# Products that nobody reads, issued in TensorE's planned pauses

## The chip, the cores and the metric

The kernel runs on one core of a Trainium2 chip. The metric is the device time of one launch in microseconds (us); the reference point is the median of three runs. A core has five engines that run side by side, each taking its own instructions in order: TensorE (PE; its weight loads are the row PEld), VectorE (DVE), ScalarE (ACT), GpSimd (POOL) and SyncE (SP), which issues the DMAs. TensorE's clock is granted by a throttle: the profile gives it as a share of full speed.

## What is computed

A gated complex linear attention, followed by a two-layer network with a Gelu. The inputs are f32, but for `w_in` and `w_out`, which arrive as 64-bit floats; the result is f32:

```python
q, k, v, a_re, a_im: (4, 8, 768, 48)          # batch, heads, time, head_dim
mag = sqrt(a_re**2 + a_im**2); scale = minimum(mag, 0.999) / (mag + 1e-6)
for t in range(768):                          # S: (4, 8, 48, 48), complex
    S = (a_re + 1j * a_im)[t] * scale[t] * S  # row by row
    S.real += k[t] outer v[t]
    y[t] = q[t] @ S.real
x = y as (3072, 384)
out = gelu(x @ w_in) @ w_out                  # (384, 2048), (2048, 384)
```

## The kernel before

**The work has four kinds of parts**, all written as steps into one plan.

- *Lanes.* The decays are normalised and multiplied up along time, in 24 slices over four groups of time steps. This is mostly VectorE's and ScalarE's, with the tiles `a`, `tab`, `bt`, `tt` and `xt`. The scaled keys and queries go through DRAM (`kq`). In the first slices TensorE adds up the squares (`sum_of`: `att<-tab` and `att<-a`).
- *Weights.* 32 pieces of 384 columns. The inputs are 64-bit floats, and each piece is split into a high part (`wi_hi`, `wo_hi`) and a low part (`wi_lo`, `wo_lo`). TensorE forms the low part in PSUM, as `ident * wh - hi - lo`: three products, the first in f32, in the profile `po<-wh,ident_r`, `po<-wi_hi,minus` and `po<-wi_lo,minus` (or the same with `wo`). ScalarE or VectorE copies the sum out (`wi_lo<-po`). The PSUM tile is always the same one, columns 0 to 383 of `pos[2]`. The next piece's first product can start when the copy is over. The buffers `wh` are two.
- *Units.* 24 of them, each 128 time steps of one batch: keys and queries are turned by TensorE (`att<-ident_r,kqn`), copied out (`kp`, `qT`), multiplied to scores (`att<-qT,kp`), masked by VectorE (`kp<-att,causal`) and multiplied with `vn`; the state is brought forward with products of 64 by 64 (`ph<-vn,kqn`). At its end ScalarE (`xT`, `x`) and VectorE split the unit's output into high and low parts. Ahead of unit 0, and as steps of unit 0, TensorE turns the ends of the first lane group (`gains`: `att<-ident_r,vw`).
- *Blocks.* Nine blocks j0 to j8 of two or three units (256 or 384 columns): the two layers, each as three products of high and low parts (`ph<-xT,wi_hi`, `po<-wo_hi,gh` and so on), with two Gelus per tile on ScalarE (`gh`, `gf`) and their difference on VectorE (`gl`).

**PSUM** has eight banks, all taken: three `att`, two `ph`, three `po` (`pos`). Block j0 has two units and uses `pos[0]` and `pos[1]`; block j1 has three and uses `pos[2]` too. A weight piece and a block's sum take 384 of a bank's 512 columns.

**The order.** Nothing of the order is written by hand. `Plan.add` records each step with its cost on its engine, and with the steps that it must follow. `Plan.order` runs through the steps forward and backward with these costs, keeps the best order, and leaves in each step its engine, the start that the plan gives it (`s.start`, us) and its cost (`s.cost`). `Plan.issue` then emits the instructions of all engines in that order. In the plan TensorE's cost doubles for 4 us (`WARM`) behind a pause of over 3 us (`COLD`). The waits between engines are put in when the program is built, from which instruction reads or writes what, in program order.

The plan's times are estimates; on the chip each engine runs its instructions as soon as what they wait for is there. A pause in the plan is the difference between one TensorE step's `s.start` and the end of the step before it on TensorE.

## Time and profile before

| | |
|---|---|
| median of 3 runs | 697.37 us (697.04 to 699.15) |
| the profiled execution | 697.16 us, of which the span of its instructions 695.1 us |
| mean granted TensorE clock | 0.957 |
| busy over the span | TensorE 92%, weight loads 85%, VectorE 67%, ScalarE 66%, GpSimd 5% |
| chain that ended last | TensorE 75%, ScalarE 11%, VectorE 10% |

How to read it: every helper's instruction carries the line of `Plan.issue` (L399), so groups are told apart by their tiles, `out<-in`. `x2` counts instructions; an f32 product is two of them, a product of the rounded kind (fp32r) one. In a time-line each row has the start, the busy time, the engine, the operation with its tiles and sizes, and in brackets the idle time ahead of it and what ended it. In a table of windows each row has the stretch, its length, then for TensorE, weight loads, VectorE, ScalarE and GpSimd the busy us and the number of instructions, then the granted clock, the DMA share and GB/s. A matmul's end is modelled, so consecutive rows of TensorE can overlap; the spacing of their starts is the better measure.

### The profile page before, as it was taken

To read this page: it belongs to the slowest core of one execution; us is meant where nothing else is said; L and a number is where in the kernel's file an instruction comes from. 1 tells how busy PE (TensorE), PEld (TensorE's weight loads), DVE (VectorE), ACT (ScalarE), POOL (GpSimd) and SP (SyncE) were. 2 spreads that over 40 slices of the span, in tenths; PEclk is the share of its full clock that TensorE was granted. 3 is DMA by queue.
4 is the path that set the end of the run, shared out by engine and by line. 5 is a ranking of instruction groups with operands and counts; after the bars stand their busy time and mean duration, and the time that the engine had idled before them with its cause. 6 is when DMAs were issued, how large, how long until landed. Compare 5 with 4: busy or idle time off the path is not lost.

```text
span 695.1 us, 13858 instructions
## 1 busy us (share of the span) xinstructions
PE 638.8 (92%) x5138; PEld 588.3 (85%) x5138; DVE 465.7 (67%) x1154; ACT 459.3 (66%) x1118; POOL 31.9 (5%) x73
## 2 busy tenths in 40 slices
PE   3464799998999999999999999999999999999995
PEld 1232477996889999999889999999999999999995
DVE  5999988999999999999999973442332222131111
ACT  7777867999988788889899864454344333343332
POOL 1002110020000000300000000100000000000000
PEclk9865589999999999999999999999999999999998
DMA  8446936677455546637767555202322030010000
GB/s 303 138 136 176 301 110 165 203 199 234 134 150 148 148 119 183 180 95 217 206 198 212 118 133 149 83 20 72 113 76 61 5 103 1 1 44 4 24 1 26
DMA packets 112713, 86.68 MB, mean 125 GB/s; under 512 B 55680, under 2 KB 104960, under 8 KB 112640
## 3 DMA queue, kind: packets, MB, share of 16 engines
q1 hardware_dynamic: 112640, 85.75, 43.3%
q8 instruction: 41, 0.67, 0.4%
q14 instruction: 32, 0.26, 0.1%
HBM read 56.82 MB, written 23.59 MB: 116 GB/s over the span
## 4 chain that ended last, share of the span: by engine, by line
PE 75%; ACT 11%; DVE 10%; issue 2%; DMA 1%; SPq 0%; ACTq 0%; DVEq 0%
PE po L399 28%; PE ph L399 26%; PE att L399 20%; DVE a L399 2%; ACT tab L399 2%; DVE tt L399 1%; ACT wh L399 1%; ACT a L399 1%; DVE wh L399 1%; DVE xt L399 1%; ACT L399 1%; ACT L397 1%; DVE bt L399 1%; DVE tab L399 1%; ACT gh L399 1%
## 5 line engine op out<-in xcount | busy, mean ns | idle before, releaser
L399 PE MATMUL ph<-xT,wi_hi 128*128 128x384 f32 (+1 forms) x864 | 210.9, 326 | 0.3 <-ACT gf L399 0.3
L399 DVE TENSOR_TENSOR gl<-gf,gh 128x384 fp32r<-128x384 f32 (+1 forms) x143 | 72.9, 510 | 137.4 <-ACT gf L399 134.7
L399 PEld LDWEIGHTS ph<-xT,wi_hi 128*128 128x128 f32 x864 | 153.0, 188 | 3.1 <-ACT gf L399 0.6
L399 ACT ACTIVATE gh<-ph 128x384 fp32r<-128x384 f32 (+1 forms) x144 | 65.5, 455 | 134.3 <-PE ph L399 133.3
L399 PE MATMUL ph<-xT,wi_lo 128*128 128x384 f32 (+1 forms) x432 | 137.2, 318 | 1.8 <-ACT wi_lo L399 1.8
L399 PE MATMUL po<-wo_hi,gh 128*128 128x384 f32 x384 | 133.0, 346 | 1.1 <-ACT gh L399 0.9
L399 PE MATMUL po<-wo_lo,gh 128*128 128x384 f32 x384 | 129.6, 338 | 0.0
L399 PE MATMUL po<-wo_hi,gl 128*128 128x384 f32 x384 | 92.1, 341 | 0.3 <-DVE gl L399 0.3
L399 PEld LDWEIGHTS ph<-xT,wi_lo 128*128 128x128 f32 x432 | 81.2, 188 | 2.0 <-ACT wi_lo L399 2.0
L399 PEld LDWEIGHTS po<-wo_hi,gh 128*128 128x128 f32 x384 | 72.1, 188 | 3.4 <-ACT gh L399 2.5
L399 PEld LDWEIGHTS po<-wo_lo,gh 128*128 128x128 f32 x384 | 72.3, 188 | 0.1
L399 DVE TENSOR_TENSOR tt<-bt,a 128x192 f32<-128x192 f32 x192 | 69.0, 360 | 0.8
L399 PEld LDWEIGHTS po<-wo_hi,gl 128*128 128x128 f32 x384 | 65.9, 188 | 1.3 <-DVE gl L399 0.9
L399 ACT ACTIVATE gf<-ph 128x384 f32<-128x384 f32 (+1 forms) x144 | 65.0, 452 | 2.1 <-DVE gl L399 1.8
L399 PE MATMUL po<-wh,ident_r 128*128 128x384 f32 x64 | 35.4, 642 | 24.7 <-ACT wh L399 8.8
L399 PE MATMUL att<-qT,kp 96*128 96x128 f32 x384 | 53.4, 283 | 2.9 <-ACT kp L399 1.0
L399 DVE TENSOR_TENSOR kp<-att,causal 128x512 f32<-128x512 f32 x48 | 33.0, 687 | 30.8 <-PE att L399 30.0
L399 PEld LDWEIGHTS att<-qT,kp 96*128 96x128 f32 x384 | 48.8, 194 | 5.1 <-ACT qT L399 1.7
L399 DVE TENSOR_TENSOR bt<-tt 128x96 f32<-128x96 f32 x192 | 48.3, 251 | 0.9
L399 PEld LDWEIGHTS po<-wh,ident_r 128*128 128x128 f32 x64 | 12.6, 233 | 30.5 <-ACT wh L399 8.7
L399 PE MATMUL att<-ident_r,kqn 128*96 128x128 f32 x384 | 35.6, 237 | 0.3 <-DVE kp L399 0.2
L399 PEld LDWEIGHTS att<-ident_r,kqn 128*96 128x96 f32 x384 | 32.6, 127 | 3.1 <-DVE kp L399 0.5
(161 smaller groups left out, 1001.3 us busy)
## 6 DMA issues: line engine op xcount, KB each, us to landing
kqn<-kq SPq DMA_DIRECT2D x24, 768.0 KB, 5.1
xt<-in_x_lanes_dram SPq DMA_DIRECT2D x24, 384.0 KB, 3.7
kq<-xt SPq DMA_DIRECT2D x48, 192.0 KB, 3.8
kq<-xt SPq DMA_DIRECT2D x24, 384.0 KB, 4.1
a<-in_a_lanes_dram SPq DMA_DIRECT2D x20, 384.0 KB, 3.7
raw<-in_w_pieces_dram SPq DMA_DIRECT2D x16, 384.0 KB, 4.0
raw<-in_moe_w_out_dram SPq DMA_DIRECT2D x16, 384.0 KB, 3.9
vn<-in_v_units_dram SPq DMA_DIRECT2D x24, 256.0 KB, 5.4
```

What stands on the lines that cost most here:

```text
L397: self.nc.scalar.preload_act_table_set(table)
L399: getattr(getattr(self.nc, engine), name)(*args, **kw)
```

## The change

Three constants are new, and `issue` takes a function `unread`. As it walks through the order, it looks at each TensorE step whose planned start is later than `first`, until the first step of block j1. `first` is the planned start of the first TensorE step of the kind "units", less 14 us. Ahead of such a step it issues as many unread products as go into the planned pause, less 0.1 us, at 0.23 us each. A product is the f32 identity times itself, 128 by 128, added to columns 384 to 511 of `pos[2]`. These are set to zero once by VectorE, ahead of everything that the plan issues, and nothing reads them. The order of the other instructions on each engine stays as it was.

```diff
+SPARE, UNREAD, LEAD = 0.1, 0.23, 14.0
...
-    def issue(self):
+    def issue(self, unread):
+
+        free, early = 0.0, True
+        order = self.order()
+        first = min(s.start for s in order if s.engine == "tensor" and s.kind == "units") - LEAD
         table = FIRST_TABLE
         self.nc.scalar.preload_act_table_set(table)
-        for s in self.order():
+        for s in order:
             if s.table and s.table != table:
                 table = s.table
                 if table != "gelu":
                     self.nc.scalar.preload_act_table_set(table)
+            if s.engine == "tensor":
+                early = early and s.part != "j1"
+                for _ in range(int((s.start - free - SPARE) / UNREAD) if early and s.start > first else 0):
+                    unread()
+                free = s.start + s.cost
             for engine, name, args, kw in s.calls:
                 getattr(getattr(self.nc, engine), name)(*args, **kw)
...
-    P.issue()
+
+    unread = pos[BLK - 1][:, DM:512]
+    nc.vector.memset(unread, 0.0)
+    P.issue(lambda: nc.tensor.matmul(out=unread, lhsT=ident[:], rhs=ident[:], start=False, stop=False, skip_group_check=True))
```

## The prediction

> **What bounds the kernel now.** I read the cores first, then the windows of 10 us (for each engine the busy microseconds, then the granted TensorE clock, the DMA share, GB/s), then the time-lines of TensorE, ScalarE and VectorE around the first unit.

> ```profile
> core 0: 695.1 us, clock 0.957
> 0.00:10.00 10.00, 1.23 (x3) 0.84 (x3) 2.85 (x7) 8.83 (x21) 2.15 (x18) 1.00 0.78 265
> 60.00:70.00 10.00, 5.03 (x12) 2.55 (x10) 9.96 (x26) 7.77 (x19) 3.44 (x3) 0.50 0.73 202
> 70.00:80.00 10.00, 5.83 (x11) 2.67 (x10) 9.66 (x31) 7.48 (x21) 2.50 (x5) 0.50 1.01 291
> 80.00:90.00 10.00, 9.07 (x86) 7.69 (x87) 8.92 (x23) 8.73 (x21) 0.00 (x0) 0.50 0.75 237
> 90.00:100.00 10.00, 10.00 (x100) 7.37 (x99) 8.83 (x16) 5.88 (x16) 2.23 (x1) 0.88 0.24 73
> 130.00:140.00 10.00, 10.00 (x97) 8.59 (x96) 9.93 (x27) 9.84 (x23) 0.47 (x2) 1.00 0.43 120
> 200.00:250.00 50.00, 49.45 (x482) 46.92 (x482) 49.52 (x127) 43.42 (x98) 0.00 (x0) 1.00 0.58 152
> ```

> The reader is to see three stages. To about 88 us VectorE has no time free (9.96 and 9.66 of 10) and TensorE half of its time. From 80 to 100 TensorE is full, at half clock for most of it. From 130 TensorE and VectorE are both full, so a shift of both at 120 us should reach the end nearly whole, and a shift of one alone should not.

> Why the clock is low: TensorE works on weight pieces (one f32 product of 384 columns and two corrections each) with pauses between them.

> ```profile
> 49.86 2.93 PE L399 MATMUL att<-a,ident_r 128*128 128x384 f32 x4 [5.12 <-ACT a L399]
> ...
> 58.71 1.65 PE L399 MATMUL po<-wh,ident_r 128*128 128x384 f32 x2 [3.22 <-ACT wo_lo L399]
> 64.11 1.65 PE L399 MATMUL po<-wh,ident_r 128*128 128x384 f32 x2 [2.88 <-ACT wi_lo L399]
> 66.20 0.63 PE L399 MATMUL att<-ident_r,vw 128*96 128x128 f32 x2
> 68.92 1.62 PE L399 MATMUL po<-wh,ident_r 128*128 128x384 f32 x2 [2.10 <-DVE wh L399]
> 70.66 0.59 PE L399 MATMUL po<-wi_lo,minus 128*128 128x384 f32 x1
> 74.26 1.65 PE L399 MATMUL po<-wh,ident_r 128*128 128x384 f32 x2 [3.00 <-ACT wi_lo L399]
> 76.02 0.52 PE L399 MATMUL po<-wo_lo,minus 128*128 128x384 f32 x1
> 77.11 1.65 PE L399 MATMUL po<-wh,ident_r 128*128 128x384 f32 x2 [0.57 <-ACT wo_lo L399]
> 80.93 1.65 PE L399 MATMUL po<-wh,ident_r 128*128 128x384 f32 x2 [1.53 <-ACT wi_lo L399]
> 83.15 1.95 PE L399 MATMUL ph<-vn,kqn 64*64 64x48 f32 x32
> 87.92 2.07 PE L399 MATMUL att<-qT,kp 96*128 96x128 f32 x8
> 89.65 1.20 PE L399 MATMUL att<-ident_r,kqn 128*96 128x128 f32 x8
> ```

> I call the six pieces P1 (58.71), P2, P3, A (74.26), B and C. Five of the six pauses end with ScalarE's copy of the piece before out of its PSUM bank. VectorE pays for the low clock in these waits:

> ```profile
> 78.11 0.36 DVE L399 TENSOR_SCALAR wh<-raw 128x384 uint32<-128x384 uint32 x1 [0.34 <-ACT wh L399]
> 90.10 0.69 DVE L399 TENSOR_TENSOR kp<-att,causal 128x512 f32<-128x512 f32 x1 [1.12 <-PE att L399]
> 94.54 0.69 DVE L399 TENSOR_TENSOR kp<-att,causal 128x512 f32<-128x512 f32 x1 [0.80 <-PE att L399]
> 95.76 0.95 DVE L399 TENSOR_TENSOR m<-st,gg 96x768 f32<-96x768 f32 x1 [0.27 <-PE ph L399]
> 117.69 0.55 DVE L399 COPY st<-att 96x384 f32<-96x384 f32 x1 [1.69 <-PE att L399]
> ```

> All five are 4.2 us, and the four behind unit 0's start 3.9. Faster TensorE work cannot give more than this before 120 us: VectorE has nothing else to save.

> **The change part by part.** The memset of 128 columns is one VectorE instruction ahead of the lanes; VectorE works 2.85 of its first 10 us, so nothing. No DMA is added, nothing is moved, and nothing is queued on SP or POOL.

> Price of one product (f32, 128 by 128, two instructions as all f32 products here): the nearest rows are the scores, four products in eight instructions. At half clock the next work starts 1.73 us behind (87.92 to 89.65), 0.43 each; at full clock:

> ```profile
> 106.51 0.91 PE L399 MATMUL po<-wh,ident_r 128*128 128x384 f32 x2
> 107.71 0.43 PE L399 MATMUL ph<-qT,st 96*48 96x64 f32 x8
> 108.66 1.12 PE L399 MATMUL att<-qT,kp 96*128 96x128 f32 x8
> 109.72 1.13 PE L399 MATMUL ph<-vn,kqn 64*64 64x48 f32 x32
> ```

> 1.06 us, 0.265 each. The change counts 0.23, so a filled pause runs over by a seventh, and at half clock by nearly its own length. The first two rows give a piece at full clock, 1.20 us (106.51 to 107.71); at half clock it is 2.28 (74.26 to 76.54).

> How many: the pauses come from the plan, which the trace shows only through its outcome. "First unit" in the code is the first TensorE step of kind units; that is the transposes of the ends at 66.20, not the products at 83.15. 14 us before it is 52.2, so all six pauses are filled. With the measured pauses (pause less 0.1, by 0.23) they get 13, 12, 8, 12, 2 and 6, together 53. The upper end: a plan that counts pieces near 1.20 us has five pauses longer by some 1.1, 4 to 5 products each, some 76.

> Where they run: the products write columns 384 to 511 of the bank whose columns 0 to 383 hold the weight pieces. What two engines do in other columns of one bank is ordered here, as a unit's split shows: VectorE's xT reads columns 0 to 383 and needs only ScalarE's xT, yet it starts when ScalarE's read of columns 384 to 511 (x) is over:

> ```profile
> 562.84 0.49 ACT L399 ACTIVATE xT<-att 128x384 fp32r<-128x384 f32 x1 [1.74 <-PE att L399]
> 563.32 0.27 ACT L399 ACTIVATE x<-att 128x128 fp32r<-128x128 f32 x1
> 563.48 0.20 ACT L399 ACTIVATION_READ_ACCUMULATOR x<-att 128x1 f32 x1
> 563.71 0.56 DVE L399 TENSOR_TENSOR xT<-att,xT 128x384 fp32r<-128x384 f32 x1 [2.02 <-ACT x L399]
> ```

> So I take it that products issued ahead of a piece wait for ScalarE's copy of the piece before, the very event that ends the pause in five of six. They run behind the pause, and the piece is queued behind them. [...]

> What waits for the pieces is ScalarE, which takes its instructions in order:

> ```profile
> 63.60 0.46 ACT L399 CAST wi_lo<-po 128x384 fp32r<-128x384 f32 x1
> 66.89 0.46 ACT L399 CAST wo_lo<-po 128x384 fp32r<-128x384 f32 x1
> 73.75 0.45 ACT L399 CAST wi_lo<-po 128x384 fp32r<-128x384 f32 x1
> 75.94 0.58 ACT L399 ACTIVATE wh<-raw 128x384 f32<-128x384 f32 x1 [0.23 <-PE po L399]
> 78.85 0.56 ACT L399 ACTIVATE wh<-raw 128x384 f32<-128x384 f32 x1 [0.77 <-ACT wh L399]
> 80.41 0.46 ACT L399 CAST wi_lo<-po 128x384 fp32r<-128x384 f32 x1
> ```

> P1: the clock stands at 0.50 there, and the share of 0.88 from 90 to 100 puts its return at 92.4, 4.5 us behind the first full work of unit 0 (the scores at 87.92). So 10 products at 0.43 and 3 at 0.265 are 5.1 us, then 1.20: it ends at 65.0, and its copy stood at 63.60; ScalarE is 1.4 late. P2: 12 products are 3.2, the piece is 1.1 shorter, its copy at 66.89 has 0.5 of slack behind its end near 66.4 (the transposes behind it start at 66.20): 1.6 more, 3.0. P3: 8 are 2.1, and from its end at 71.25 to its copy at 73.75 there are 2.5: nothing. A: 12 are 3.2; the activation at 75.94 had waited for A's first product, 0.75 shorter at full clock: 2.4 more, 5.4. B: 2 are 0.5, against the same 0.75 at 78.85: 0.2 back, 5.2. C: 6 are 1.6, less 1.1: unit 0 starts 5.7 late, near 88.9. VectorE waits for ScalarE's wh at 78.11 already, so it is late with it: 5.2 less that 0.34, about 4.9. (Were VectorE's buffers to hide it all, this term would be zero; with the clock at half throughout, 53 products at 0.43 less those slacks would make it about 15.)

> What comes back is unit 0 at full clock: its 6.85 us from 83.15 to about 90.0 become 4.1 to 4.6 (the ratio of 1.73 to 1.06, and a little for ScalarE's copies between), so the scores are there at about 93.5, and VectorE, late itself, arrives at 93.9 (its wait began at 88.98, 90.10 less 1.12). The waits of 1.12, 0.80, 0.27 and, if the clock holds until then, 1.69 go: 3.9. What is late next is VectorE's own queue.

> From unit 0 to the second block more planned pauses are filled. The lower end is nothing, where a pause is real; the upper is 0.265 for each product where TensorE has no pause, as from 130 to 140. The pause left out of account by 0.1 and the seventh of overrun make a few tenths for each; I take five products, 1.3.

> Sum: 4.9 - 3.9 + 1.3 = 2.3 us on the profiled execution's 697.16, 699.4. That execution stands 0.2 under the median of the three runs, 697.37.

> **The rivals.** First, other side: the products do not wait for the copy and run inside the pauses. Then the 4.9 is gone and all 4.2 are gained, less overruns, of which I keep 1.2: 694.2. For it speaks that every pause is there in the trace and VectorE is full; against it the rows at 563. It decides if fewer than about half of the products before C stand behind the copies, since 3.9 then outweighs 2.5 and 1.3.

> Second: the plan's pauses are the long ones. 23 products more, 6.1 us, of which the slack of P3 and B's and C's waits take about 2: 703.5. The same comes out if 14 us before the transposes reaches the step at 49.86 too.

> Third: the products do run, but the clock does not hold through unit 0. TensorE was 9.07 of 10 us busy from 80 to 90 and stayed at 0.50, on transposes and 64 by 64 products. Without the 3.9 the time is 697.16 + 4.9 + 1.3 = 703.4. [...]

> Fourth: the filled pauses change nothing, TensorE being off the path until 74 us: delay and gain cancel, 697.2.

> **How the numbers follow.** A measurement of this kernel tells about 0.3% (2.1 us) from no change. The main case has 0.50; its own range is 697.3 to 701.5, half of it above 699.5: 0.25 slower, 0.25 within. The first rival has 0.27, all faster, 692.5 to 695.2. The second and third have 0.09 and 0.08, slower. The fourth has 0.06, within. So 0.27 faster, 0.31 same, 0.42 slower. The range reaches from inside the first rival to the second: 693.3 to 703.5.

> **What would show it.** Right: clock 1.00 from about 63 to past 120; products starting behind wi_lo and wo_lo, and the next piece right behind them; P1's copy near 65.0, A's activation near 81, unit 0's first product near 88.9; VectorE's waits near 90 to 97 and at 117 gone. Wrong: products that start at the end of the piece before; unit 0 at 83 or earlier; a clock of 0.50 anywhere from 65 to 120; TensorE late at the second block by more than VectorE.

## The result, and the profile after

The changed kernel takes 705.9 us (median of 4 runs, 704.79 to 708.95) against 697.67 (4 runs) for the kernel before: a ratio of 1.0122, with a 95% interval of 1.0085 to 1.0159, 8.2 us more. The forecast was 699.4.

The profiled execution, of 708.95 us, is the longest of the four, so shifts read from it are some 3 us larger than the median's. Its lines have the number L409 where the kernel before has L399, and the added products are L1026. Its cores view and some of its windows:

```profile
core 0: 706.8 us, clock 0.967
60.00:70.00 10.00, 9.43 (x60) 8.39 (x58) 7.67 (x20) 4.61 (x11) 3.38 (x2) 0.84 0.60 167
70.00:80.00 10.00, 6.76 (x53) 6.05 (x53) 8.56 (x25) 7.28 (x20) 2.11 (x5) 1.00 0.89 246
80.00:90.00 10.00, 7.66 (x31) 5.96 (x29) 5.59 (x19) 4.24 (x14) 0.00 (x0) 0.66 0.88 272
90.00:100.00 10.00, 9.27 (x124) 8.59 (x124) 7.50 (x19) 7.82 (x18) 0.00 (x0) 1.00 0.22 60
120.00:130.00 10.00, 9.17 (x79) 7.29 (x79) 7.77 (x20) 7.16 (x21) 0.00 (x0) 0.83 0.69 188
200.00:250.00 50.00, 49.46 (x494) 45.62 (x495) 49.45 (x127) 43.39 (x98) 0.00 (x0) 1.00 0.58 150
```

The clock came early, as wanted: 0.84 and 1.00 where it was 0.50. But the third busy column, VectorE's, fell from 9.96, 9.66 and 8.92 to 7.67, 8.56 and 5.59 between 60 and 90 us: VectorE, which had 1.5 us of these 30 free, now stands for 8. From 80 to 90 us the clock was lost again (0.66). From 200 us on the rows are alike. The mean clock rose from 0.957 to 0.967 and the span by 11.7.

TensorE's time-line shows why (start, busy us, tiles, number of instructions, and the idle time ahead with what ended it):

```profile
59.45 6.29 PE L1026 MATMUL po<-ident_r 128*128 128x128 f32 x38 [2.98 <-ACT wo_lo L409]
65.58 0.81 PE L409 MATMUL po<-wh,ident_r 128*128 128x384 f32 x2
...
67.31 1.83 PE L1026 MATMUL po<-ident_r 128*128 128x128 f32 x14 [0.57 <-ACT wi_lo L409]
...
70.88 4.51 PE L1026 MATMUL po<-ident_r 128*128 128x128 f32 x38 [0.75 <-ACT wo_lo L409]
75.22 0.38 PE L409 MATMUL att<-ident_r,vw 128*96 128x128 f32 x2
...
79.09 1.86 PE L1026 MATMUL po<-ident_r 128*128 128x128 f32 x12 [2.49 <-ACT wi_lo L409]
...
83.44 3.78 PE L1026 MATMUL po<-ident_r 128*128 128x128 f32 x16 [0.57 <-ACT wo_lo L409]
...
90.02 2.27 PE L1026 MATMUL po<-ident_r 128*128 128x128 f32 x18 [1.79 <-ACT wi_lo L409]
...
93.12 0.83 PE L1026 MATMUL po<-ident_r 128*128 128x128 f32 x6
93.89 1.14 PE L409 MATMUL ph<-vn,kqn 64*64 64x48 f32 x32
```

The pauses are still there, in the brackets. The products stand behind them, each group behind ScalarE's copy out of the same bank, and the piece behind the products. Two instructions are one product: 19, 7, 19, 6, 8, 9 and 3, together 71 ahead of unit 0. Fifteen more follow by block j0 (2 and 3 in unit 0, 1 near 120 us, 6 and 3 in block j0). Unit 0 starts at 93.89, not 83.15.

ScalarE's and VectorE's time-lines show who waits for the late pieces:

```profile
66.78 0.48 ACT L409 CAST wi_lo<-po 128x384 fp32r<-128x384 f32 x1 [2.33 <-PE po L409]
82.27 0.56 ACT L409 ACTIVATE wh<-raw 128x384 f32<-128x384 f32 x1 [2.21 <-PE po L409]
```

```profile
68.89 0.56 DVE L409 TENSOR_TENSOR a<-a 128x384 f32<-128x384 f32 x1 [2.28 <-ACT a L409]
77.76 0.56 DVE L409 TENSOR_TENSOR a<-tab,a 128x384 f32<-128x384 f32 x1 [1.05 <-ACT a L409]
79.68 0.36 DVE L409 TENSOR_SCALAR wh<-raw 128x384 uint32<-128x384 uint32 x1 [0.40 <-ACT wh L409]
84.44 0.36 DVE L409 TENSOR_SCALAR wh<-raw 128x384 uint32<-128x384 uint32 x1 [2.32 <-ACT wh L409]
89.64 0.36 DVE L409 TENSOR_SCALAR wh<-raw 128x384 uint32<-128x384 uint32 x1 [2.09 <-ACT wh L409]
95.07 0.55 DVE L409 COPY st<-ph 96x384 f32<-96x384 f32 x1 [1.48 <-PE ph L409]
99.93 0.69 DVE L409 TENSOR_TENSOR kp<-att,causal 128x512 f32<-128x512 f32 x1 [1.02 <-PE att L409]
123.02 0.69 DVE L409 TENSOR_TENSOR kp<-att,causal 128x512 f32<-128x512 f32 x1 [1.23 <-PE att L409]
126.99 0.55 DVE L409 COPY st<-att 96x384 f32<-96x384 f32 x1 [1.00 <-PE att L409]
```

TensorE is late, so ScalarE's copy is late, so ScalarE's next work for the lanes (`a`) and the weights (`wh`) is late, and VectorE waits for it: the first seven waits are 10.6 us, where the kernel before had 2.5 in this stretch (0.34, 1.12, 0.80 and 0.27). The last two are 2.2, where it had 1.69.

### The profile page after: what moved, and what is told of

It is laid out like the page before. It is cut to its first block, busy times and chain, and to the rows that moved or that the text cites. A ratio compares the mean times of both kernels' runs of the same rounds, so it can differ in the third digit from the quotient of the medians.

```text
span 706.8 us, 14195 instructions
## 1 busy us (share of the span) xinstructions
PE 655.3 (93%) x5310; PEld 608.0 (86%) x5310; DVE 466.2 (66%) x1155; ACT 459.4 (65%) x1118; POOL 31.6 (4%) x73
## 4 chain that ended last, share of the span: by engine, by line
PE 74%; DVE 12%; ACT 8%; issue 3%; DMA 2%; SPq 1%; DVEq 0%; ACTq 0%
PE po L409 27%; PE ph L409 25%; PE att L409 18%; PE po L1026 3%; DVE a L409 3%; DVE tt L409 2%; ACT wh L409 2%; ACT tab L409 1%; ACT a L409 1%; DVE xt L409 1%; DVE bt L409 1%; DVE tab L409 1%; DVE gl L409 1%; DVE kp L409 1%; DVE wh L409 1%
## 5 line engine op out<-in xcount | busy, mean ns | idle before, releaser
L409 PE MATMUL ph<-xT,wi_hi 128*128 128x384 f32 (+1 forms) x864 | 211.3, 326 | 0.3 <-ACT gf L409 0.3
L409 DVE TENSOR_TENSOR gl<-gf,gh 128x384 fp32r<-128x384 f32 (+1 forms) x143 | 73.0, 510 | 136.9 <-ACT gf L409 134.0
L409 PEld LDWEIGHTS ph<-xT,wi_hi 128*128 128x128 f32 x864 | 153.2, 188 | 3.1 <-ACT gf L409 0.6
L409 ACT ACTIVATE gh<-ph 128x384 fp32r<-128x384 f32 (+1 forms) x144 | 65.6, 456 | 132.9 <-PE ph L409 131.9
L409 PE MATMUL ph<-xT,wi_lo 128*128 128x384 f32 (+1 forms) x432 | 137.2, 318 | 0.0
L409 PE MATMUL po<-wo_hi,gh 128*128 128x384 f32 x384 | 132.9, 346 | 0.9 <-ACT gh L409 0.7
L409 PE MATMUL po<-wo_lo,gh 128*128 128x384 f32 x384 | 129.6, 338 | 0.0
L409 PE MATMUL po<-wo_hi,gl 128*128 128x384 f32 x384 | 92.2, 341 | 0.3 <-DVE gl L409 0.3
L409 PEld LDWEIGHTS ph<-xT,wi_lo 128*128 128x128 f32 x432 | 81.4, 188 | 0.0
L409 PEld LDWEIGHTS po<-wo_hi,gh 128*128 128x128 f32 x384 | 72.1, 188 | 3.0 <-ACT gh L409 2.1
L409 PEld LDWEIGHTS po<-wo_lo,gh 128*128 128x128 f32 x384 | 72.3, 188 | 0.1
L409 DVE TENSOR_TENSOR tt<-bt,a 128x192 f32<-128x192 f32 x192 | 69.2, 361 | 0.8
L409 PEld LDWEIGHTS po<-wo_hi,gl 128*128 128x128 f32 x384 | 65.9, 188 | 1.3 <-DVE gl L409 0.9
L409 ACT ACTIVATE gf<-ph 128x384 f32<-128x384 f32 (+1 forms) x144 | 65.2, 452 | 2.1 <-DVE gl L409 2.0
L409 PE MATMUL att<-qT,kp 96*128 96x128 f32 x384 | 53.1, 282 | 1.1 <-DVE kp L409 0.9
L409 DVE TENSOR_TENSOR kp<-att,causal 128x512 f32<-128x512 f32 x48 | 33.0, 688 | 31.4 <-PE att L409 30.9
L409 PEld LDWEIGHTS att<-qT,kp 96*128 96x128 f32 x384 | 48.6, 193 | 3.0 <-ACT kp L409 1.1
L409 DVE TENSOR_TENSOR bt<-tt 128x96 f32<-128x96 f32 x192 | 48.4, 252 | 0.9
L409 PE MATMUL po<-wh,ident_r 128*128 128x384 f32 x64 | 31.5, 578 | 12.6 <-ACT wh L409 8.8
L1026 PE MATMUL po<-ident_r 128*128 128x128 f32 x172 | 26.6, 317 | 13.2 <-ACT wi_lo L409 8.2
L1026 PEld LDWEIGHTS po<-ident_r 128*128 128x128 f32 x172 | 24.4, 224 | 15.9 <-ACT wi_lo L409 9.6
L409 PE MATMUL att<-ident_r,kqn 128*96 128x128 f32 x384 | 34.8, 234 | 0.3 <-DVE kp L409 0.2
```

Of the source, the lines that this page charges most:

```text
L409: getattr(getattr(self.nc, engine), name)(*args, **kw)
L1026: P.issue(lambda: nc.tensor.matmul(out=unread, lhsT=ident[:], rhs=ident[:], start=False, stop=False, skip_group_check=True))
```

## The experiments

Each ratio is to the kernel before on the same chip, with its 95% interval. The theory under test: the products cost time because they queue behind a copy out of their own bank, and there are more of them than the measured pauses hold; a clock that is kept through unit 0 gives some 4 us back. The main rivals: the products themselves cost the time, wherever they write; or the clock does not hold anyway.

This table has the starts of unit 0's first product and of blocks j0 and j1 in the profiled execution of each kernel. "Back" is how much of unit 0's delay against the kernel before is gone at j0. It is one execution each. e7 adds nothing ahead of j0, yet 1.3 is gone there: the wait of 1.69 us at 117.69 in the kernel before, whose clock is 0.83 from 110 to 120 us, is missing in e7, whose clock is 1.00 there. e3 and the same kernel once more, e11, have 0.9 and 2.8. So a difference under 2 in this column says nothing.

| kernel | unit 0 | j0 | j1 | back | ratio |
|---|---|---|---|---|---|
| before | 83.15 | 118.67 | 194.39 | | |
| after | 93.89 | 127.96 | 206.03 | 1.4 | 1.0122 |
| e1 ahead only | 91.57 | 123.88 | 200.10 | 3.2 | 1.0089 |
| e2 from unit 0 only | 83.64 | 122.11 | 200.10 | -3.0 | 1.0059 |
| e3 ahead, other bank | 82.35 | 116.97 | 193.22 | 0.9 | 0.9978 |
| e4 e3 and the rest | 84.07 | 118.45 | 196.42 | 1.1 | 1.0017 |
| e5 predicted counts | 90.93 | 124.92 | 200.65 | 1.5 | 1.0071 |
| e6 one each | 85.37 | 120.92 | 196.65 | 0.0 | 0.9994 |
| e7 one pause of j0 | 84.36 | 118.58 | 195.15 | 1.3 | 1.0017 |
| e8 clock through unit 0 | 83.62 | 115.14 | 190.88 | 4.0 | 0.9953 |
| e9 last pauses only | 85.11 | 116.62 | 192.58 | 4.0 | 0.9966 |
| e10 transposes | 88.27 | 121.03 | 196.84 | 2.8 | 1.0028 |
| e11 e3 again | 83.87 | 116.61 | 192.73 | 2.8 | 0.9983 |
| e12 e8 again | 83.43 | 115.43 | 191.16 | 3.5 | 0.9948 |

### e1 and e2: the two halves

e1 keeps the products ahead of unit 0's first product, e2 the others; `ahead` ends with that step.

```diff
+                n = int((s.start - free - SPARE) / UNREAD) if early and s.start > first else 0
-                for _ in range(int((s.start - free - SPARE) / UNREAD) if early and s.start > first else 0):
+                for _ in range(n if ahead else 0):        # e2: 0 if ahead else n
                     unread()
+                ahead = ahead and not (s.kind == "units" and s.form == "narrow")
```

> Products only ahead of unit 0's first product (68 of them in seven pauses), in the same bank as in the changed kernel; none from there on. Theory A (the loss is made ahead of unit 0, by products queued behind ScalarE's copy out of their bank): unit 0's first product stays near 93.9 us (83.15 before) and the time stays 6 to 9 us above the kernel before, 703.5 to 707. Rival C (the loss is made by the products from unit 0 on): at most 2 us above the kernel before, under 700.

Measured: 704.23 against 697.3, ratio 1.0089 (1.006 to 1.0118).

> Products only from unit 0's first product to the second block (18), none ahead. Theory A: within 2 us of the kernel before, 696 to 700, unit 0's first product at 83.2 us. Rival C: 703 or more.

Measured: 702.19 against 697.3, ratio 1.0059 (1.0041 to 1.0078). This is a miss: the fifteen products (the expectations of e1 to e4 count 18 and 68 where there are 15 and 71) cost 4 to 5 us, where at most 2 were expected. e2's time-line of TensorE shows where:

```profile
86.40 1.17 PE L1028 MATMUL po<-ident_r 128*128 128x128 f32 x4
87.50 1.95 PE L411 MATMUL po<-vn,kqn 64*64 64x48 f32 x32
89.37 1.65 PE L1028 MATMUL po<-ident_r 128*128 128x128 f32 x6
90.81 1.91 PE L411 MATMUL att<-qT,kp 96*128 96x128 f32 x8
162.44 1.79 PE L1028 MATMUL po<-ident_r 128*128 128x128 f32 x12 [1.99 <-ACT wi_lo L411]
```

In unit 0, at half clock (0.50 from 80 to 90 us, 0.73 from 90 to 100), there is no pause ahead of the products: two take 1.10 us (86.40 to 87.50) and three 1.44 (to 90.81), all on the path. By the table the nine in j0 cost 2.3 (3.4 late at j0, 5.7 at j1). With one near 115 us the sum is about 5. The two halves make 1.0148 together, inside the interval of the whole.

### e3 and e11: the same products in a bank that no one copies from meanwhile

e1's products in columns 384 to 511 of the second `ph` bank. e11 is the same kernel on another chip.

```diff
-    unread = pos[BLK - 1][:, DM:512]
+    unread = ph[1][:, DM:512]
```

> The same 68 products ahead of unit 0 in the same places of TensorE's queue, but written into a ph bank, which no engine reads before unit 0; none from there on. They wait for nothing. Theory A: they run when the piece before them ends, most of them inside the pauses; unit 0 starts at 82 to 85 us, the waits of VectorE near 90 to 97 go, 694.5 to 697.5. Rival B (too many products at too low a price, wherever they run): P1's 19 and the transposes' 19 overrun their pauses by 2 to 5 us each, unit 0 starts at 88 or later, 701 or more.

Measured: 696.18 against 697.3, ratio 0.9978 (0.9962 to 0.9995).

> The run with the other bank once more, beside the next one on the same chip: 0.998 of the kernel before.

Measured: 697.76 against 698.25, ratio 0.9983 (0.9966 to 1.0). e3's time-line of TensorE and its windows:

```profile
65.43 4.40 PE L1028 MATMUL ph<-ident_r 128*128 128x128 f32 x38
69.67 0.38 PE L411 MATMUL att<-ident_r,vw 128*96 128x128 f32 x2
82.35 1.14 PE L411 MATMUL ph<-vn,kqn 64*64 64x48 f32 x32
87.27 2.08 PE L411 MATMUL att<-qT,kp 96*128 96x128 f32 x8 [2.04 <-ACT qT L411]
```

```profile
80.00:90.00 10.00, 7.96 (x104) 7.20 (x103) 9.19 (x23) 8.47 (x21) 0.00 (x0) 0.81 0.77 249
90.00:100.00 10.00, 10.00 (x95) 7.03 (x94) 8.38 (x16) 5.79 (x16) 2.23 (x1) 0.85 0.20 60
```

The 71 products run in the pauses, without a bracket, and unit 0 starts at 82.35. One line of code makes 8.05 us (704.23 against 696.18 on one chip): the products do not cost the time, their place behind the copy does. But the clock is lost again, near 86 us, where unit 0's scores wait 2.04 us for ScalarE's `qT`, and part of the gain goes with it: 1.5 us by the ratio, where e8 below has 3.3. In e11 the wait is 1.26 us, and the clock is 0.86 from 90 to 100. The 19 products at 65.43 take 4.24 us to the next start, 0.223 each.

### e4: e3, and the fifteen later products where the change has them

```diff
-                for _ in range(n if ahead else 0):
-                    unread()
+                for _ in range(n):
+                    unread(int(ahead))                    # 1: ph[1], 0: pos[BLK - 1]
```

> As the run before, and the 18 products from unit 0 on in the changed kernel's bank. Theory A: the later ones cost or bring little, 694 to 699; if they hold the clock through 112 to 116 us (0.50 in the kernel before), up to 1.7 us less than the run before, otherwise up to 2 us more.

Measured: 699.29 against 697.3, ratio 1.0017 (0.9999 to 1.0035): 3.1 us above e3, where at most 2 were expected. The later products' cost did not go away with the higher clock (a mean of 0.972 in its profiled execution, 0.945 in e2's).

### e5 and e6: the number of products, in the change's own bank

```diff
+        counts = iter((13, 12, 8, 12, 2, 6, 0))           # e6: (1,) * 7
...
+                if n:
+                    n = next(counts, 0)
```

> Products only ahead of unit 0, in the changed kernel's bank, with the counts that the prediction worked with: 13, 12, 8, 12, 2 and 6 instead of 19, 7, 19, 6, 8, 9 and 3. If the ledger of the prediction was right and only its counts were off: 1 us above the kernel before, 697 to 700 (late by 4.9, 3.9 back). If what comes back was also put too high: 701 to 703, with VectorE's waits on TensorE between 90 and 118 us still there.

Measured: 703.2 against 698.82, ratio 1.0071 (1.0048 to 1.0093). VectorE's time-line:

```profile
84.29 0.36 DVE L413 TENSOR_SCALAR wh<-raw 128x384 uint32<-128x384 uint32 x1 [4.20 <-ACT wh L413]
97.22 0.69 DVE L413 TENSOR_TENSOR kp<-att,causal 128x512 f32<-128x512 f32 x1 [1.21 <-PE att L413]
102.39 0.69 DVE L413 TENSOR_TENSOR kp<-att,causal 128x512 f32<-128x512 f32 x1 [1.54 <-PE att L413]
```

With the predicted counts the delay is near the predicted one: unit 0 at 90.93, less 1.3 for an execution that was that much later already at 53 us, is 6.5 late (predicted 5.7). What fails is the other term: the waits for the scores are still there, 1.21 and 1.54, and the clock was lost again ahead of unit 0 and in it (0.84 from 80 to 90 us, 0.67 from 90 to 100).

> One product in each of the seven pauses ahead of unit 0, in the changed kernel's bank: the wait on ScalarE's copy stays, the queue behind it is 0.27 to 0.43 us. Theory A (what costs is the products queued behind the copy, not the wait, which the next piece has anyway): 696.5 to 698.5, no change. Rival (the additional wait or the shared bank costs by itself): 700 or more.

Measured: 698.7 against 698.82, ratio 0.9994 (0.9973 to 1.0016). Its time-line of TensorE, at P1:

```profile
59.21 0.80 PE L1030 MATMUL po<-ident_r 128*128 128x128 f32 x2 [3.23 <-ACT wo_lo L413]
59.80 1.49 PE L413 MATMUL po<-wh,ident_r 128*128 128x384 f32 x2
```

The piece starts 0.59 behind the product. A wait as such costs nothing, since the piece had the same one; the length of the queue behind it does.

### e7: one pause of block j0

```diff
-                for _ in range(n):
+                for _ in range(n if s.kind == "blocks" or s.kind == "units" and s.part != "u0" and s.start > first + 100 else 0):
```

> Six products in a single pause of block 0 (near 159 us, where TensorE waits 1.8 us for ScalarE's wi_lo and is full otherwise), in the changed kernel's bank; none elsewhere. Theory A: they run behind that copy at 0.27 to 0.30 each, with nothing to take it up: 1.6 to 1.9 us above the kernel before, 698.7 to 699.4. If the planned pause hid them: no change.

Measured: 699.78 against 698.82, ratio 1.0017 (0.9993 to 1.0042). The interval holds both answers. The time-line of TensorE says what the time cannot:

```profile
159.38 1.60 PE L1027 MATMUL po<-ident_r 128*128 128x128 f32 x12 [2.00 <-ACT wi_lo L410]
160.75 0.48 PE L410 MATMUL ph<-xT,wi_hi 128*128 128x256 f32 x2
```

The six products are issued ahead of a pause and run behind it, and the block's next product comes 1.4 us behind their start. Not all of that stays: by the table e7 is 0.1 early at j0 and 0.8 late at j1. The changed kernel and e2, with three products more in j0, lose 2.3 from j0 to j1, but there the clock falls too (0.97 from 140 to 200 us, 1.00 in e7). So what six products cost in a full block is not settled; by this trace it is less than the 1.6 to 1.9 expected.

### e8 and e12: the clock held through unit 0

All in the `ph` bank: the change's own groups ahead of unit 0, in unit 0 two and five (it had two and three), none later. e12 is the same kernel on another chip.

```diff
+        counts = iter((19, 7, 19, 6, 8, 9, 3, 2, 5))
...
-    unread = pos[BLK - 1][:, DM:512]
+    unread = ph[1][:, DM:512]
```

> As the run with the other bank, and 2 and 5 products more in unit 0, in that same bank, in the pauses ahead of its second 64 by 64 products and of its scores (2.0 us of waiting for ScalarE's qT there). Theory: the clock, which the run with the other bank lost for 6.8 us from about 86 us, holds, the scores run at 0.27 each, VectorE's waits of 0.81 and 1.35 shrink: 0.5 to 1.5 us less than that run, 694.5 to 696. If transposes and 64 by 64 products pull the clock down all the same: as that run or up to 0.5 more.

Measured: 694.63 against 698.82, ratio 0.9953 (0.9933 to 0.9973).

> The run that held the clock through unit 0 once more: 0.995 of the kernel before, 0.2 to 0.3% less than the run beside it; the seven products in unit 0 are all that differs.

Measured: 694.23 against 698.25, ratio 0.9948 (0.9921 to 0.9975). e12's time-line of TensorE and its windows:

```profile
86.76 1.38 PE L1030 MATMUL ph<-ident_r 128*128 128x128 f32 x10
88.36 1.16 PE L413 MATMUL att<-qT,kp 96*128 96x128 f32 x8 [0.22 <-ACT qT L413]
```

```profile
80.00:90.00 10.00, 9.78 (x128) 8.84 (x127) 10.00 (x27) 9.29 (x24) 0.00 (x0) 1.00 0.83 261
90.00:100.00 10.00, 10.00 (x110) 7.68 (x110) 10.00 (x21) 6.38 (x18) 2.23 (x1) 1.00 0.45 133
110.00:120.00 10.00, 9.82 (x127) 8.10 (x129) 9.92 (x28) 8.73 (x24) 0.00 (x0) 1.00 0.70 202
```

Five products fill the wait for `qT` at which e3 lost its clock; with the two ahead of them they are all that differs. The clock is 1.00 in all three rows, and VectorE is busy 10.00 of 10 us at 80 and at 90: not one wait for TensorE is left from 50 to 125 us. Block j0 starts 3.2 us earlier than in the kernel before (e8: 3.5), and the time is 3.3 to 4.2 less. The interval lies below 1 on two chips, so this version is faster than both kernels, by about half a per cent.

### e9: the last pauses only

e8 with `(0, 0, 0, 0, 8, 9, 3, 2, 5)`.

> As the run that held the clock through unit 0, but without the products in the first four pauses: 8, 9 and 3 ahead of unit 0 (from about 77 us) and 2 and 5 in it, all in the ph bank. Theory: TensorE's work from about 77 us on without a break grants the clock by 81 to 84 us, VectorE loses nothing before, so most of the gain is there: 695 to 696.5. If the clock must come earlier for VectorE's sake: within 0.5 us of the kernel before.

Measured: 696.48 against 698.25, ratio 0.9966 (0.9949 to 0.9984). Its windows:

```profile
70.00:80.00 10.00, 6.98 (x23) 5.14 (x23) 9.65 (x31) 6.78 (x19) 2.55 (x5) 0.50 1.01 300
80.00:90.00 10.00, 10.00 (x125) 9.12 (x125) 9.02 (x24) 8.83 (x23) 0.00 (x0) 0.99 0.77 239
```

Without the 51 products of the first four groups the clock is up from 80 us, and "back" is 4.0 as in e8. So most of the gain is that of the clock in unit 0. The intervals of e9 and e12 overlap, and what the first groups add is not settled.

### e10: transposes in the place of products

e8 with four rounded transposes for each product.

```diff
-    unread = ph[1][:, DM:512]
+    unread = ph[1][:, DM:512].bitcast(F32R)
...
-    P.issue(lambda: nc.tensor.matmul(out=unread, lhsT=ident[:], rhs=ident[:], start=False, stop=False, skip_group_check=True))
+    P.issue(lambda: [nc.tensor.transpose(out=unread, in_=ident_r[:], identity=ident_r[:]) for _ in range(4)])
```

> As the run that held the clock through unit 0, with each product replaced by four transposes of the identity (0.3 us together at full clock), in the same places and the same bank. If transposes count as work for the clock: as that run, clock 1.00 from 60 to 120 us. If they do not: the clock stands near 0.50 as in the kernel before, the pauses are overrun by half, and the time is 697 to 701.

Measured: 701.22 against 698.25, ratio 1.0028 (1.0006 to 1.0051). Its windows, and rows of its time-line of TensorE:

```profile
56.00:59.00 3.00, 3.00 (x26) 3.00 (x25) 2.98 (x10) 2.88 (x9) 0.04 (x1) 0.51 0.65 175
60.00:70.00 10.00, 10.00 (x104) 9.40 (x102) 9.36 (x24) 6.80 (x17) 3.39 (x2) 1.00 0.65 172
80.00:90.00 10.00, 10.00 (x123) 9.27 (x122) 8.82 (x24) 7.76 (x20) 0.00 (x0) 1.00 0.79 238
```

```profile
55.76 7.72 PE L1030 MATMUL ph<-ident_r 128*128 128x128 f32 x76
...
64.38 2.53 PE L1030 MATMUL ph<-ident_r 128*128 128x128 f32 x28
66.74 0.88 PE L413 MATMUL po<-wh,ident_r 128*128 128x384 f32 x2
```

The clock answers: it rises during the first group, and is 1.00 from 60 to 130 us, on transposes and short pieces. The time does not, because 28 transposes take 2.36 us to the next start, 0.34 for four against 0.223 for a product: the pauses overflow, and unit 0 starts 5.1 late.

## Why the prediction was wrong

**Right: the mechanism.** Products wait for ScalarE's copy of the same bank and run behind the pause; the next piece queues behind them; ScalarE and then VectorE are late. e1 and e3 differ in the bank alone: the added products wait for ScalarE six times in the one (9.2 us) and never in the other. That agrees with the rows at 563 us that the prediction went by. The clock did rise at 63.2 us (0.50 from 62 to 63 us, 0.89 from 63 to 64, 1.00 from 64 to 80), and products start behind `wi_lo` and `wo_lo`. The fourth rival (nothing changes) is out, and so is the first (no wait) for this bank. Its 694.2 is nearly what e8 and e12 measure (694.63, 694.23), but that is in part luck: they have seven products more in unit 0, and e3, where the products run in the pauses as that rival has it, measures 696.18.

By the prediction's own terms the part ahead of unit 0 should have cost 4.9 - 3.9 = 1.0 us, and the later part 1.3.

**Wrong, first: what comes back.** e5 has the predicted counts and none of the later products, so it should have cost that 1.0; its ratio on 698.82 is 5.0 us. VectorE's rows say which term failed. In this table "ready" is the time at which VectorE is free for unit 0's first mask (the start of its first `kp<-att,causal`, less the wait). "Late" is how far that is behind the kernel before, less what the execution was late already at 53 us. "Back" is how much of the whole lateness is gone when VectorE starts `st<-att`, at 117.69 in the kernel before. It is one execution each.

| kernel | ready | late at 53 us | late | `st<-att` | back |
|---|---|---|---|---|---|
| before | 88.98 | | | 117.69 | |
| predicted | | | 4.9 | | 3.9 |
| after | 98.91 | 0.7 | 9.2 | 126.99 | 0.6 |
| e1 ahead only | 96.58 | 0.1 | 7.5 | 122.90 | 2.4 |
| e5 predicted counts | 96.01 | 1.3 | 5.7 | 123.94 | 0.8 |
| e7 nothing ahead | 90.18 | 1.2 | 0.0 | 117.48 | 1.4 |
| e8 clock through unit 0 | 89.08 | 0.0 | 0.1 | 114.17 | 3.6 |
| e12 e8 again | 89.65 | 1.3 | -0.6 | 114.44 | 3.9 |

In e5 the delay is near the predicted one, 5.7 for 4.9, but of the 3.9 only 0.8 comes back. Where the clock is 1.00 through unit 0 and its waits are filled, as in e8 and e12 (1.00 from 80 to 100 us in e12; means of 0.983 and 0.985), 3.6 and 3.9 do come back. So the term was right in size under its condition, and the step that failed is the condition: that unit 0 runs at full clock and VectorE, late itself, no longer waits for it. The prediction named the sign, a clock of 0.50 between 65 and 120 us, and it came (0.50 from 80.5 to 87.0 us in the changed kernel). In e5 the clock is lost again ahead of unit 0 and in it, and VectorE's waits are still there. That is the third rival's outcome, but not by transposes: with them as filler the clock held in e10 (1.00 from 60 to 130 us).

In the changed kernel's profiled execution the term fails in another way. The clock is 1.00 from 90 to 120 us, yet VectorE waits 1.48 and 1.02 us for unit 0, which is 10.7 late where 5.7 were predicted and has five added products in it. Then the product at 120.83 waits 1.32 us, the clock falls (0.83 from 120 to 130), and VectorE waits 1.23 and 1.00 more. That is 4.7 us, where the kernel before waits 3.9.

A part of the 3.9 was luck from the start. The wait of 1.69 at 117.69, counted as something to win, is missing in e7 as well, where nothing is added ahead of it.

**Wrong, second: the later products.** Five at 0.265, 1.3 us, were taken; there were fifteen, for 4.1 us by e2's ratio (2.9 to 5.4), 2.8 more. The prediction named the upper end, the full price wherever TensorE has no pause, and that end, 4.0 for fifteen, is what they cost in e2; its five of unit 0 even ran at half clock (0.50 from 80 to 90 us).

**Wrong, third: the number ahead of unit 0.** The prediction took the pauses of the trace for those of the plan and counted 13, 12, 8, 12, 2 and 6, together 53. The program counts by the plan: 71, near the 76 of the upper end, with 19 each ahead of P1 and of the transposes. P1's copy came at 66.78 instead of 65.0, A's activation at 82.27 instead of near 81, unit 0 at 93.89 instead of 88.9 (0.7 of each is an execution that was later already at 53 us). By the ratios of e1 and e5 this made 1.3 us, but their intervals overlap, so it is not shown to be more than noise. By VectorE's rows e1 is 7.5 late and e5 5.7. The changed kernel has the same products ahead as e1 and is 9.2 late: B's eight take 3.57 us in it (83.44 to 87.01), at a clock of 0.50, and 1.89 in e1, whose clock is 0.86 from 80 to 90 us. The second rival's 703.5 is near e1's 704.23, but its reason, the number, carries only that part.

**Price.** 0.265 for a product was a little high: 0.223 in e3, 0.237 behind a wait in after (7 from 67.31 to 68.97), both at a clock of 1.00. The change's 0.23 is about right there.

**The sum again.** By the ratios: 2.3 forecast, 4.0 that e5 cost more, 2.8 and 1.3 are 10.4; measured are 8.2, with an interval from 5.9 to 11.1. By the rows of the profiled execution: 0.7 from the start, 9.2 late at unit 0, 0.6 back and 2.3 in block j0 (9.3 late at j0, 11.6 at j1) are 11.6 of its 11.7. Why it is 3 us above the median stays open: the other three executions have no trace. Their mean clocks are 0.970, 0.972 and 0.976 in the order of falling time, where it has 0.967.

## What to carry to other kernels

Filler for a pause must wait for nothing that ends the pause: put it into a bank that no engine reads meanwhile, or, as here, it runs behind the pause and the next piece queues behind it (1.0089 in e1, 0.9978 in e3, whose bank alone differs). Look at the pauses that the chip shows, since a plan's estimate can be far from them (53 and 71 products here), and leave filler out where the engine is full. A clock is worth only what waits for its work: e10 held 1.00 from 60 to 130 us and its ratio is 1.0028. Here the 27 products from the last pauses to the short wait inside unit 0 (e9, 0.9966) carried most of the gain (0.9948 in e12), and what the first 51 add is not settled.
